# One Mish activation from PSUM in the second mixture, and small VectorE work of the attention on other engines

## The chip, the cores and the metric

The kernel runs on one core of a Trainium2 chip. Its five engines run side by side, each with its own queue that is worked in order: TensorE (PE in the profile; its weight loads are PEld), VectorE (DVE), ScalarE (ACT), GpSimd (POOL) and SyncE (SP), whose queue issues all the transfers here. The metric is device microseconds of one execution; lower is better.

## The reference

Three layers follow each other. B=2, H=8, S=768, D=40, so 1536 tokens of 320 values; the weights come as float64.

```python
for t in range(S):                                   # attention with gates, per batch and head
    m_new = max(f_gate[t] + m, i_gate[t])
    f_stab, i_stab = exp(f_gate[t] + m - m_new), exp(i_gate[t] - m_new)
    C = f_stab * C + i_stab * outer(v[t], k[t])
    n = f_stab * n + i_stab * k[t]
    y[t] = sigmoid(o_gate[t]) * (C @ q[t]) / max(abs(n . q[t]), 1)
x = ((y @ w1) * (y @ w2)) @ w3 @ w_out               # first mixture, 320 -> 1024 -> 320
h = x @ w_in                                         # second mixture, 320 -> 2048 -> 320
out = (h * tanh(softplus(h))) @ w_out2               # h * tanh(softplus(h)) is Mish
```

## The kernel before

**Precision.** Every float32 operand of a large product is split into a high part, rounded to the type that TensorE multiplies at full rate, and a low part, the rest. A product is high x high + high x low + low x high, summed in PSUM. So each activation tile needs a rounding copy and a subtraction.

**Weights.** A weight piece is 128 rows by up to 384 columns of float64 words; there are 80. Each is a chain over four engines (`add_piece`): SP loads the words (`raw`, 4 buffers); `mag` (ACT, an Abs over the high words, L285); `clamp`, `bits1`, `bits2`, `bits` (four DVE passes that put a float32 together, L289, L293, L298, L303); `hi` (ACT rounding copy, L308); `lo` (POOL subtraction, L211, the line of a helper `tt` that issues every two-input operation). The float32 in the middle, `f`, has 5 buffers.

**Attention.** Chunks of 128 steps; a unit `u` is one chunk of all 8 heads of one batch, 12 units. Per unit: `E` (PE exponents) -> `dw` (ACT exp) -> `vw` (POOL) ; `S` (PE scores) -> `wg` (DVE); `I` (PE, what the state gives) -> `Ie` (DVE); `U` (PE) -> `st` (DVE, new state); `Y` (PE) -> `cb`, `r1`, `r2`, `r3` (DVE: sum, magnitude, max with 1, reciprocal) -> `xo` (POOL, three operations) -> `X` (PE transpose) -> `Xe` (ACT), `Xl` (DVE, two operations: low parts). `rb(c)` builds the right-hand factor of the exponents of chunk c on DVE, once per chunk, and `E` waits for it. Products without a use (`keep_warm`, tile `psz`, L369) stand at the start and in the first five units, since TensorE's granted clock falls when it has little to do.

**First mixture.** Tokens stand in 3 blocks of 512. Per block and each of 8 slices of 128 columns: `A` and `B` (8 products of 512 columns each, L747, tiles `psa`, `psb`), `Ae` (ACT copy), `Be` (DVE product of both), `Ph` (ACT), `Pl` (DVE), then `X1` (8 products, L787 to L792, tile `psx`). `W` (L721, tile `psw`) multiplies w3 by w_out beforehand.

**Second mixture.** 48 steps i (3 blocks x 16 slices of 128 columns). `H` (8 products of 512 columns, L747, tile `psh`) -> `He` (copy of PSUM to `h`, the first 18 on ACT, L844, the rest on DVE, L846) -> `Hm` (DVE min with 20, L849) -> `Hx` (ACT Exp, L852) -> `G`, for two steps at a time (ACT Ln of 1 + u for both, L909, then Tanh for both, L911; a load of ScalarE's function table ahead of each pair) -> `gm` (DVE product with `h`), `gh` (DVE rounding copy, L859), `gl` (DVE subtraction) -> `O` (12 products of 320 columns, L874, tile `pso`).

**Order.** `Work` is a list scheduler that runs while the kernel is built: every node has an engine, a due number, a duration that it is thought to last, what it depends on and the buffer places that it takes; on a free engine the node that can start first, and among such the one that is due first, comes next. The due numbers come from `TUNE`. The result is a fixed order in each queue.

Of the kernel before, what the change touches and what calls it, by code (L numbers as in the profile page):

```python
# [10 lines left out]
F32 = mybir.dt.float32  # L11
# [5 lines left out]
# numbers of buffers  # L17
# [8 lines left out]
NUH = 22  # L26
NG_ = 3
GRP = 2
# where the streams of work stand in the order
TUNE = dict(  # L30
    s_pe=0.21, s_act=0.25, s_dve=0, s_pool=0.02, warm=5, ahead=6, w0n=10, he_act=18, a0=132.2, ap=2.52,
    a_ld=-24.1, e_e=289.88, e_s=231.89, e_r=475.63, rb=6, g_ld=-373.09, o_1=-239.57, o_2=520.41, c_ld=-47.15,
    c_wo=548.73, cp_wo=0.032, p0=141.8, pp0=6.543, c_12=-449.5, w0=-140.23, wp=0.004, t_0=-366.73,
    c_w3=-109.65, p1=-597.93, pp1=0.013, p2=-192.0, pp2=621.703, x0=337.71, x_p=-433.57, x1=51.37, x2=-134.49,
    xp=0.002, c_o2=449.63, cp_o2=0.01, c_wi=511.67, c_o3=121.71, m0=987.19, mp0=0.005, mp=1.376, m_o=15.52,
    m_g=228.41, m_t=218.91,
)

# the magnitudes of float32 as the high words of float64, read as float32
# [4 lines left out]
class Work:  # L44
    """Orders the work of the engines: nodes with what they depend on, the places that they take and how long they
    are thought to last; on a free engine the node that is due first comes next."""
# [3 lines left out]
    TABLE = 1.3  # L50
    WINDOW = 3.4133
# [27 lines left out]
    def run(self, t0, fill=None):  # L79
# [15 lines left out]
        def place_of(takes, got):  # L95
            """the place of a list that is free first, or None if none is known to be"""
# [13 lines left out]
        while left:  # L110
# [65 lines left out]
def kernel(  # L176
# [69 lines left out]
    # places of 2 KiB in each partition, the first of them from the start  # L246
# [22 lines left out]
    pieces = []  # L269

    def add_piece(due, lead, width, loads, outs, takes=(), gates=()):
        """outs: functions that give the tiles of the high and the low part, in the places that takes names"""
# [37 lines left out]
        def low():  # L310
# [4 lines left out]
        add_node(("mag", n), "ACT", due - 4, 0.41 * e, mag, [("load", n), ("mag", n - 1)],  # L315
                 [(places("f", NF), [("lo", n)])])
# [8 lines left out]
    def cols_loads(w, ft):  # L325
        """128 columns of a matrix with 384 rows"""
# [28 lines left out]
    # the factors of the exponents, whose rows are high and low parts of 16 rows of gates each  # L355
# [4 lines left out]
    def load_rows(dst, src, u):  # L360
        """the rows of a unit, all heads of one time step side by side"""
# [3 lines left out]
    def keep_warm(n):  # L365
        """products without a use: the tensor engine's clock falls when its array has little to do"""
# [4 lines left out]
    def add_unit(u, due):  # L371
# [10 lines left out]
        def ld_qk():  # L382
            """the columns of a unit, the heads in pairs at partitions 0 and 64"""
# [66 lines left out]
        def state():  # L450
# [43 lines left out]
        def xo():  # L494
# [4 lines left out]
            nc.gpsimd.tensor_copy(out=x[:, DM:3 * T], in_=x[:, R0:DM])  # L499
# [11 lines left out]
        def Xl():  # L511
# [3 lines left out]
            tt(nc.vector, h[64:128, 2, sl], p3[64:128, 2], h[64:128, 2, sl].bitcast(F32), sub)  # L515
# [5 lines left out]
        node("E", "PE", -K["e_e"], 0.87, E, [("lb", int(c > 0)), ("rb", c), ("E", u - 1)],  # L521
             [at("dw"), at("dw"), (places("w", NW), [("Y", u), ("vw", u)])])
        node("dw", "ACT", -K["e_e"] + 1, 0.96, dw, [("E", u)], table=["exp"])
        node("S", "PE", -K["e_s"], 1.75 + wl, S_, [("ld_qk", u), ("E", u), ("Y", u - K["ahead"])], [at("wg"), at("wg")], warm=wl)
        node("wg", "DVE", -3, 1.2, wg, [("S", u), ("dw", u), ("vw", u)])
        if c > 0:
            node("I", "PE", -2, 0.87, inter, [("ld_qk", u), ("st", u - B), ("rb", c)],
                 [(AT, [("Ie", u), ("dx", u)] if more else [("Ie", u)])], warm=0.0)
            node("Ie", "DVE", -1, 0.41, inter_e, [("I", u), ("turn", 1)], [(places("y", 2), [("xo", u)])])
        if more:  # L530
# [4 lines left out]
            node("st", "DVE", -1, 1.0 if c else 0.5, state, [("U", u), ("I", u), ("dx", u)])  # L535
        node("Y", "PE", 0, 1.75 + wl, Y, [("wg", u), ("ld_kv", u)], [at("cb")], warm=wl)
        node("cb", "DVE", 1, 0.41, cb, [("Y", u), ("Ie", u)], [] if c else [(places("y", 2), [("xo", u)])])
        node("r1", "DVE", 1, 0.08, r1, [("cb", u)], [(places("r", 2), [("xo", u)])])
        node("r2", "DVE", 1, 0.08, r2, [("r1", u)])
        node("r3", "DVE", 1, 0.12, r3, [("r2", u)])  # L540
        node("xo", "POOL", 2, 2.0, xo, [("r3", u), ("sgm", kb * B + b)], [(places("x", 2), [("X", u)])])
        node("X", "PE", 3, 0.33, X, [("xo", u)], [at("Xl")], warm=0.0)
        node("Xe", "ACT", 3, 0.37, Xe, [("X", u), ("set", kb)])
        node("Xl", "DVE", 3, 0.54, Xl, [("Xe", u)])
# [23 lines left out]
    def start():  # L568
        G = B * H
        # they stand where the activations come later; the rows of the gates eight times, those of sixteen at 32 n used  # L570
# [37 lines left out]
        def part(c0, c1):  # L608
            """the gates of some chunks: what the exponentials are made of"""
# [22 lines left out]
        def rb(c):  # L632
            e = nc.vector if c < K["rb"] else nc.gpsimd
            sl = slice(c * T, (c + 1) * T)
            tt(e, ex_r[c % 2][64:128], L2[64:128, sl].bitcast(F32).unsqueeze(1).to_broadcast([64, H, T]),
# [45 lines left out]
        for c in range(NCH):  # L681
            add_node(("rb", c), "DVE" if c < K["rb"] else "POOL", K["a0"] + 2 * c * K["ap"] - K["e_r"], 1.13 if c < K["rb"] else 1.86,
# [20 lines left out]
    def add_w3(i, due, due_c):  # L703
# [20 lines left out]
        def Wh():  # L724
            w = w34[r] = w34_tile(r, "w34")
            nc.scalar.copy(w[:, 0:R0], tr[r][:, 0:R0])
            nc.scalar.copy(w[:, 512:512 + R], tr[r][:, R0:DM])

        def Wl():
            w = w34[r]  # L730
            tt(nc.vector, w[:, R0:2 * R0], tr[r][:, 0:R0], w[:, 0:R0].bitcast(F32), sub)
            tt(nc.vector, w[:, 512 + R:640], tr[r][:, R0:DM], w[:, 512:512 + R].bitcast(F32), sub)

        add_node(("W", i), "PE", due, 0.406 * n, W,
                 [("lo", w3_n[i]), ("W", i - 1), *[("lo", wo_n[c0 + c]) for c in range(n)]],
                 [(WB, [("Wl", r)])] if ci == 0 else [])
        if ci == NC3 - 1:
            add_node(("Wh", r), "ACT", due + 1, 0.37, Wh, [("W", i)])
# [279 lines left out]
```

## Time and profile before

| | us |
|---|---|
| median of 3 runs | 475.64 (474.40 to 475.76) |
| span of the profiled execution | 478.8 |
| PE busy / PEld busy | 456.2 / 391.3 |
| DVE busy | 399.6 |
| ACT busy | 295.8 |
| POOL busy | 127.7 |
| mean granted TensorE clock | 0.918 |

The profile holds no separate device time for its execution; its span, from the first instruction to the last, is 3.2 us above the median of the runs. Busy time is the union of an engine's instructions; overlapping matmuls make a busy PE look fuller than it is. The granted clock is given as a share of 2.4 GHz; a stretch at 0.50 ran at 1.2 GHz. Stretches are counted in us from the start of the span.

### The profile page before, as it was taken

How to read it: one execution, taken by the hardware profiler on the slowest of the kernel's cores; microseconds unless marked ns; L12 is line 12 of the kernel's file. 1: busy time of each engine (PE TensorE's matmuls, PEld its weight loads, DVE VectorE, ACT ScalarE, POOL GpSimd, SP SyncE). 2: the span in 40 equal slices, each digit the busy share in tenths (PEclk: the TensorE clock that was granted, in tenths of full speed). 3: DMA queues.
4: the chain of work that ended last, by engine and by line, in shares of the span. 5: the costliest groups of instructions: out<-in, count | busy, mean ns of one | idle time of the engine just before them, and what ended most of it. 6: DMA issues, size and time to landing. Idle time of an engine off the chain costs nothing.

```text
span 478.8 us, 7146 instructions
## 1 busy us (share of the span) xinstructions
PE 456.2 (95%) x2490; PEld 391.3 (82%) x2490; DVE 399.6 (83%) x809; ACT 295.8 (62%) x513; POOL 127.7 (27%) x141
## 2 busy tenths in 40 slices
PE   6999899899899999999999998987999999999997
PEld 4777788788787798988888886776887889999996
DVE  5988996998969668777698886999599988878874
ACT  7453245423226542244355649997799899999990
POOL 3345264452245222232212221226241100000000
PEclk9669655958979999999999999989899999999999
DMA  7915454443412332233323332324120000001001
GB/s 215 288 53 161 149 172 139 124 126 94 126 34 88 120 111 88 89 93 93 98 60 120 100 100 67 100 73 115 50 82 1 27 30 0 1 1 56 0 2 55
DMA packets 31828, 41.93 MB, mean 88 GB/s; under 512 B 2160, under 2 KB 25968, under 8 KB 31792
## 3 DMA queue, kind: packets, MB, share of 16 engines
q1 hardware_dynamic: 31792, 41.48, 28.5%
q8 instruction: 19, 0.31, 0.3%
q14 instruction: 17, 0.14, 0.1%
HBM read 39.50 MB, written 1.97 MB: 87 GB/s over the span
## 4 chain that ended last, share of the span: by engine, by line
PE 63%; DVE 19%; issue 7%; ACT 6%; POOL 2%; DMA 1%; SPq 1%; POOLq 0%; DVEq 0%; ACTq 0%
PE pso L874 12%; PE psh L747 9%; PE psa L747 8%; PE psb L747 7%; PE psw L721 6%; PE psY L471 4%; DVE f L298 3%; PE psS L422 2%; DVE f L289 2%; DVE f L303 2%; PE psz L369 2%; PE psx L788 2%; PE psx L789 2%; PE psx L787 2%; POOL wil L211 2%
## 5 line engine op out<-in xcount | busy, mean ns | idle before, releaser
L747 PE MATMUL psh<-hs,wih 128*128 128x512 f32 x144 | 57.4, 399 | 0.0
L747 PE MATMUL psh<-hs,wil 128*128 128x512 f32 x144 | 49.5, 398 | 3.1 <-POOL wil L211 3.1
L289 DVE TENSOR_SCALAR f<-f 128x384 f32<-128x384 f32 (+2 forms) x80 | 36.8, 463 | 14.0 <-ACT f L285 13.7
L303 DVE SCALAR_TENSOR_TENSOR f<-raw,f 128x384 int32<-128x384 int32 (+2 forms) x80 | 47.0, 592 | 1.0
L285 ACT ACTIVATE f<-raw 128x384 f32<-128x384 f32 (+2 forms) x80 | 41.5, 524 | 10.2 <-DMA raw<-in_w_dram 5.7
L298 DVE SCALAR_TENSOR_TENSOR f<-raw,f 128x384 int32<-128x384 int32 (+2 forms) x80 | 46.7, 589 | 0.9
L874 PE MATMUL pso<-wo,gh 128*128 128x320 f32 x192 | 42.6, 310 | 0.0
L211 POOL TENSOR_TENSOR th<-f,th 128x384 fp32r<-128x384 f32 (+1 forms) x24 | 23.6, 984 | 61.7 <-ACT th L308 51.6
L211 DVE TENSOR_TENSOR u<-u,h 128x512 f32<-128x512 f32 x48 | 35.1, 746 | 4.9 <-ACT u L911 4.9
L747 PE MATMUL psh<-ls,wih 128*128 128x512 f32 x96 | 38.4, 400 | 0.0
L211 DVE TENSOR_TENSOR gl<-u,gh 128x512 fp32r<-128x512 f32 x48 | 32.7, 686 | 4.9 <-PE pso L874 4.2
L747 PEld LDWEIGHTS psh<-hs,wil 128*128 128x128 f32 x144 | 27.7, 193 | 9.5 <-POOL wil L211 3.6
L293 DVE TENSOR_SCALAR f<-f 128x384 int32<-128x384 int32 (+2 forms) x80 | 34.2, 434 | 1.1
L471 PEld LDWEIGHTS psY<-kv,w 128*128 128x128 f32 x192 | 33.6, 256 | 1.5 <-DVE w L211 0.2
L874 PEld LDWEIGHTS pso<-wo,gh 128*128 128x128 f32 x192 | 32.6, 188 | 1.5 <-issue 0.4
L874 PE MATMUL pso<-wo2h,gl 128*128 128x320 f32 x96 | 30.8, 320 | 3.0 <-DVE gl L211 3.0
L747 PE MATMUL psa<-hs,w12h 128*128 128x512 f32 x72 | 30.4, 422 | 3.1 <-DVE hs L211 2.1
L471 PE MATMUL psY<-kv,w 128*128 128x41 f32 x192 | 33.3, 337 | 0.1
L308 ACT CAST th<-f 128x384 fp32r<-128x384 f32 (+1 forms) x24 | 11.5, 480 | 35.3 <-DVE f L303 23.9
L852 ACT ACTIVATE u<-u 128x512 f32<-128x512 f32 x48 | 28.9, 624 | 5.9 <-DVE u L849 5.6
L211 POOL TENSOR_TENSOR wil<-f,wih 128x384 fp32r<-128x384 f32 x16 | 21.5, 1356 | 41.0 <-ACT wih L308 41.0
L747 PEld LDWEIGHTS psh<-hs,wih 128*128 128x128 f32 x144 | 27.8, 193 | 5.0 <-ACT wih L308 0.2
(137 smaller groups left out, 1250.6 us busy)
## 6 DMA issues: line engine op xcount, KB each, us to landing
raw<-in_w_dram SPq DMA_DIRECT2D x32, 384.0 KB
raw<-in_w_out_dram SPq DMA_DIRECT2D x24, 320.0 KB
raw<-in_w_in_dram SPq DMA_DIRECT2D x16, 384.0 KB
kv<-in_kv_dram SPq DMA_DIRECT2D x12, 324.0 KB
qk<-in_qk_dram SPq DMA_DIRECT2D x24, 160.0 KB
raw<-in_w_dram SPq DMA_DIRECT2D x8, 256.0 KB
sg<-in_o_gate_dram SPq DMA_DIRECT2D x12, 160.0 KB
out_dram<-yo SPq DMA_DIRECT2D x12, 160.0 KB
```

The source lines that it names most:

```text
L211: return eng.tensor_tensor(out=o, in0=a, in1=b, op=op)
L285: nc.scalar.activation(out=t["f"].bitcast(F32), in_=t["raw"][:, :, 1].bitcast(F32), func=AF.Abs)
L289: nc.vector.tensor_scalar(out=ff, in0=ff, scalar1=HI_MIN, scalar2=HI_MAX, op0=ALU.max, op1=ALU.min)
L293: nc.vector.tensor_scalar(out=f, in0=f, scalar1=3, scalar2=0x3FFFFFFF, op0=ALU.logical_shift_left, op1=ALU.bitwise_and)
L298: nc.vector.scalar_tensor_tensor(out=f, in0=t["raw"][:, :, 1], scalar=-0x40000000, in1=f, op0=ALU.bitwise_and, op1=ALU.bitwise_or)
L303: nc.vector.scalar_tensor_tensor(out=f, in0=t["raw"][:, :, 0], scalar=29, in1=f, op0=ALU.logical_shift_right, op1=ALU.bitwise_or)
L308: nc.scalar.copy(t["h"], t["f"].bitcast(F32))
L471: nc.tensor.matmul(ps[:, h * VW:(h + 1) * VW], lhsT=t["w"][:, h, :], rhs=t["v"][:, h, :], start=True, stop=True)
L721: nc.tensor.matmul(ps, lhsT=t[a][:, c * 128:(c + 1) * 128], rhs=wo[b], start=(c0 + c + s == 0), stop=(c0 + c == KC - 1 and s == 2))
L747: nc.tensor.matmul(ps, lhsT=a, rhs=b, start=(n == 0), stop=(n == len(seq) - 1))
L852: nc.scalar.activation(out=t["u"], in_=t["u"], func=AF.Exp)
L874: nc.tensor.matmul(ps, lhsT=t[a][:, sl], rhs=wo[b], start=(ft == 0 and n == 0), stop=(ft == KF2 - 1 and n == 2))
```

## The change

Second mixture: `He`, `Hm`, `Hx`, `G`, `gm` and `gh` go. Two ACT activations read the bank of `H` itself: `Mh` writes Mish rounded (`gh`), `Mu` writes it in full (`u`); `gl` subtracts. The bank is free after `Mu`. The pairs of steps go too, and the places of the tiles are laid out anew (8 steps may lie between `Mh` and the end of `O`). `H` waits for the last `B` instead of the last `W`.

Weights: for the 32 pieces of the second mixture (`w_in2`, `w_out2`) `mag` is a DVE bit mask instead of an ACT Abs.

Attention: `r1` is an Abs on ACT; the two half-height products of `st` are one; the second operation of `Xl` goes, and `xo` has a fourth operation on POOL for it; `rb` of chunks 2 to 5 is 8 ACT copies with a scale, one per head, instead of one DVE product.

First mixture: the high part of w3 x w_out is one ACT copy instead of two (the same values, laid out side by side). Order: nearly all due numbers of `TUNE`, some durations of nodes, a factor 1.12 on the durations of DVE nodes, `keep_warm` at the start 10 -> 3 products, in the units 5 -> 6 units, and `S` may now run at most 2 units ahead of `Y`.

```diff
-    s_pe=0.21, s_act=0.25, s_dve=0, s_pool=0.02, warm=5, ahead=6, w0n=10, he_act=18, a0=132.2, ap=2.52,
+    s_pe=0.286, s_act=0.0, s_dve=0.0, s_pool=0.0, warm=6, ahead=2, w0n=3, a0=134.03, ap=1.26,
...
+            if e == "DVE":
+                last *= self.SHARED
...
-            nc.scalar.activation(out=t["f"].bitcast(F32), in_=t["raw"][:, :, 1].bitcast(F32), func=AF.Abs)
+            if abs_act:
+                nc.scalar.activation(out=t["f"].bitcast(F32), in_=t["raw"][:, :, 1].bitcast(F32), func=AF.Abs)
+            else:
+                nc.vector.tensor_single_scalar(out=t["f"], in_=t["raw"][:, :, 1], scalar=0x7FFFFFFF, op=ALU.bitwise_and)
...
-                for rows, e, s_e, _ in halves():
-                    tt(nc.vector, s_e, s_e, t["d"][rows, e::2].unsqueeze(2).to_broadcast([D, HP, VW]), mult)
+                s = st[b].rearrange("a p (e v) -> a (p e) v", e=2)
+                tt(nc.vector, s, s, t["d"].unsqueeze(2).to_broadcast([128, H, VW]), mult)
...
-            nc.vector.scalar_tensor_tensor(out=r, in0=y[:, :, D], scalar=-1.0, in1=y[:, :, D],
-                                           op0=mult, op1=ALU.max)
+            nc.scalar.activation(out=r, in_=y[:, :, D], func=AF.Abs)
...
-            nc.gpsimd.tensor_copy(out=x[:, DM:3 * T], in_=x[:, R0:DM])
+            nc.gpsimd.tensor_copy(out=x[:, DM:3 * T].bitcast(F32R), in_=x[:, R0:DM])
+            tt(nc.gpsimd, x[:, R0:DM], x[:, R0:DM], x[:, DM:3 * T], sub)
...
-            tt(nc.vector, h[64:128, 2, sl], p3[64:128, 2], h[64:128, 2, sl].bitcast(F32), sub)
...
-            e = nc.vector if c < K["rb"] else nc.gpsimd
+            if c >= K["rb"]:
+                for h in range(H):
+                    nc.scalar.activation(out=ex_r[c % 2][64:128, h], in_=L2[64:128, sl].bitcast(F32), func=AF.Copy,
+                                         scale=sel_h[64:128, h:h + 1])
+                return
...
-            nc.scalar.copy(w[:, 0:R0], tr[r][:, 0:R0])
-            nc.scalar.copy(w[:, 512:512 + R], tr[r][:, R0:DM])
+            nc.scalar.copy(w[:, 0:DM], tr[r][:, 0:DM])
...
-        def He():
...
-        def gh():
+        def Mh():
             t["gh"] = z_slot("gh").bitcast(F32R)
-            nc.vector.tensor_copy(out=t["gh"], in_=t["u"])
+            nc.scalar.activation(out=t["gh"], in_=t["ps"], func=AF.Mish)
+
+        def Mu():
+            t["u"] = z_slot("u")
+            nc.scalar.activation(out=t["u"], in_=t["ps"], func=AF.Mish)
...
-        add_node(("H", i), "PE", due, 1.73, Hp, [("lo", wi_n[ft]), ("X1l", kb), ("H", i - 1), ("W", KC * NC3 - 1)],
-                 [(MM, [("He", i)])])
+        add_node(("H", i), "PE", due, 1.82, Hp, [("lo", wi_n[ft]), ("X1l", kb), ("H", i - 1), ("B", NBLK * KF1 - 1)],
+                 [(MM, [("Mu", i)])])
```

## Rows read from the trace of the kernel before

**Rows 1.** Busy time by stage of the span: us of the stretch, then busy us (x instructions) of PE, PEld, DVE, ACT and POOL, the granted clock, the share of the DMA engines and GB/s. The stages are the attention, the first mixture, the second mixture up to where PE runs without gaps, and the rest.

```profile
0.00:139.90 139.90, 130.40 (x827) 107.19 (x827) 121.00 (x262) 57.43 (x110) 57.12 (x77) 0.76 0.48 144
139.90:283.20 143.30, 142.28 (x691) 121.19 (x690) 114.39 (x226) 66.94 (x148) 42.27 (x43) 1.00 0.31 94
283.20:383.50 100.30, 92.09 (x441) 78.06 (x440) 89.34 (x181) 89.46 (x148) 28.28 (x21) 0.95 0.22 68
383.50:475.50 92.00, 91.42 (x537) 84.90 (x536) 74.34 (x142) 82.01 (x108) 0.00 (x0) 1.00 0.03 10
...
sum 478.80, PE 456.20 PEld 391.33 DVE 399.60 ACT 295.85 POOL 127.67; mean PE 91.24 PEld 78.27 DVE 79.92 ACT 59.17 POOL 25.53
```

**Rows 2.** The stretch 283.20 to 383.50 again, of some products alone: first those of L747 (`H`, and one `B`), then those of tile `pso` (`O`), then those of tile `psx` (`X1`). The number behind the first x counts the products.

```profile
283.20:383.50 100.30, 59.66 (x240) 46.29 (x239) 0.95 0.22 68
...
283.20:383.50 100.30, 33.06 (x192) 30.68 (x193) 1.68 (x4) 0.95 0.22 68
...
283.20:383.50 100.30, 2.96 (x9) 1.54 (x8) 1.87 (x3) 1.65 (x3) 0.95 0.22 68
```

**Rows 3.** The chain of work that ended last, in order of time: start us, us, what.

```profile
179.14 18.17 PE psb L747 x80
...
310.87 1.28 ACT L909
312.17 1.15 ACT u L909 x2
313.37 1.25 issue
...
330.17 4.27 POOL wil L211
...
438.24 1.81 PE psh L747 x8
440.05 1.77 PE pso L874 x12
```

**Rows 4.** Who waited for whom in the stretch 283.20 to 383.50: us in total, times, longest us.

```profile
POOL wil L211 <- ACT wih L308: 36.0, 8, 6.8
...
PEld pso L874 <- DVE gl L211: 4.4, 5, 2.1
```

**Rows 5.** The stretch 283.20 to 383.50, of the instructions that write or read tile `u` alone: busy us (x instructions) of DVE and of ACT.

```profile
283.20:383.50 100.30, 45.82 (x78) 38.06 (x65) 0.95 0.22 68
```

**Rows 6.** Groups of DVE instructions in the stretch 283.20 to 383.50: busy us, mean ns of one, idle us ahead of them.

```profile
L211 DVE TENSOR_TENSOR gl<-u,gh 128x512 fp32r<-128x512 f32 x16 | 10.9, 682 | 0.3
L303 DVE SCALAR_TENSOR_TENSOR f<-raw,f 128x384 int32<-128x384 int32 (+1 forms) x21 | 10.9, 526 | 0.1
...
L293 DVE TENSOR_SCALAR f<-f 128x384 int32<-128x384 int32 (+1 forms) x20 | 8.9, 452 | 0.1
...
L846 DVE COPY h<-psh 128x512 f32<-128x512 f32 x10 | 6.8, 682 | 0.3
```

**Rows 7.** Groups of ACT instructions in the same stretch.

```profile
L909 ACT ACT_TABLE_LOAD x10 | 12.8, 1283 | 0.1
L911 ACT ACT_TABLE_LOAD x10 | 12.8, 1283 | 0.2
...
L285 ACT ACTIVATE f<-raw 128x384 f32<-128x384 f32 (+1 forms) x20 | 10.6, 528 | 0.0
...
L844 ACT COPY h<-psh 128x512 f32<-128x512 f32 x18 | 10.0, 578 | 2.3 <-PE psh L747 2.2
```

**Rows 8.** The stretches of the attention behind 20 us in which the clock was granted at 0.50; columns as in rows 1.

```profile
20.00:31.70 11.70, 11.70 (x69) 10.42 (x69) 11.49 (x22) 8.50 (x12) 2.76 (x4) 0.50 0.49 147
...
52.20:82.90 30.70, 30.70 (x158) 26.28 (x159) 26.32 (x61) 12.32 (x22) 13.14 (x17) 0.50 0.50 149
...
96.50:110.20 13.70, 13.70 (x57) 10.93 (x57) 12.48 (x25) 3.27 (x7) 5.69 (x7) 0.50 0.32 95
...
130.70:137.50 6.80, 6.80 (x26) 5.92 (x26) 6.22 (x17) 0.00 (x0) 2.59 (x5) 0.50 0.18 58
```

**Rows 9.** Groups of DVE instructions over the whole span, shapes kept apart (`rb`, the products of `st`, `r1`, `Ie`, the second operation of `Xl`).

```profile
L211 DVE TENSOR_TENSOR ex_r<-gates,sel_h 64x1024 fp32r<-64x1024 f32 x6 | 7.3, 1222 | 1.3 <-PE psI L436 1.2
L211 DVE TENSOR_TENSOR st<-st,d 40x164 f32<-40x164 f32 x16 | 7.0, 439 | 0.3
L485 DVE SCALAR_TENSOR_TENSOR r<-y 128x8 f32<-128x8 f32 x12 | 6.9, 574 | 0.1
...
L211 DVE TENSOR_TENSOR y<-psI,eT 128x328 f32<-128x328 f32 x10 | 5.0, 498 | 0.4 <-ACT d L409 0.2
...
L211 DVE TENSOR_TENSOR hs<-psX,hs 64x128 fp32r<-64x128 f32 x12 | 3.5, 294 | 0.2
```

**Rows 10.** The instructions on tile `r`, of which this is `r1`: duration in ns, least, median and most.

```profile
L485 DVE SCALAR_TENSOR_TENSOR r<-y x12: 167/773/973, 28.0 to 136.2; 128x8 f32<-128x8 f32 x12
```

**Rows 11.** Groups of the whole span, shapes kept apart, for prices of ACT and POOL: a function over 512 columns of SBUF (`Hx`), the copy in `xo`, the exponent of 8 columns, an ACT copy with a scale from a tile.

```profile
L852 ACT ACTIVATE u<-u 128x512 f32<-128x512 f32 x48 | 28.9, 624 | 5.9 <-DVE u L849 5.6
...
L499 POOL COPY x<-x 128x64 f32<-128x64 f32 x12 | 3.6, 302 | 0.8
...
L409 ACT ACTIVATE d<-psI 128x8 f32<-128x8 f32 x8 | 1.4, 178 | 6.2 <-PE psI L436 3.7 <-DVE y L211 2.5
...
L645 ACT ACTIVATE ex_l<-gates,sel_b 64x128 fp32r<-64x128 f32 x2 | 0.7, 395 | 0.0
```

More of the change, by code (lines that the diff above doesn't have):

```diff
@@ L50 @@
     TABLE = 1.3
+    SHARED = 1.12
     WINDOW = 3.4133
@@ L269, with add_piece @@
     pieces = []
-    def add_piece(due, lead, width, loads, outs, takes=(), gates=()):
+    def add_piece(due, lead, width, loads, outs, takes=(), gates=(), abs_act=True):
         n = len(pieces)
@@ L314, in add_piece @@
                  bytes=width * 1024)
-        add_node(("mag", n), "ACT", due - 4, 0.41 * e, mag, [("load", n), ("mag", n - 1)],
-                 [(places("f", NF), [("lo", n)])])
+        add_node(("mag", n), "ACT" if abs_act else "DVE", due - 4, (0.41 if abs_act else 0.35) * e, mag,
+                 [("load", n), ("mag", n - 1)], [(places("f", NF), [("lo", n)])])
         add_node(("clamp", n), "DVE", due - 3, 0.27 * e, clamp, [("mag", n)])
@@ L681, in start @@
         for c in range(NCH):
-            add_node(("rb", c), "DVE" if c < K["rb"] else "POOL", K["a0"] + 2 * c * K["ap"] - K["e_r"], 1.13 if c < K["rb"] else 1.86,
+            add_node(("rb", c), "DVE" if c < K["rb"] else "ACT", K["a0"] + 2 * c * K["ap"] - K["e_r"], 1.13 if c < K["rb"] else 2.2,
                      lambda c=c: rb(c), [("ll", int(c > 0)), ("rb", c - 1)] +
@@ L737, in add_w3 @@
         if ci == NC3 - 1:
-            add_node(("Wh", r), "ACT", due + 1, 0.37, Wh, [("W", i)])
+            add_node(("Wh", r), "ACT", due + 1, 0.4, Wh, [("W", i)])
             add_node(("Wl", r), "DVE", due + 2, 0.47, Wl, [("Wh", r)])
@@ L839, in Hp @@
             mm320(t["ps"], cols(wi_n[ft], "h"), cols(wi_n[ft], "l"), xset["b", kb])
-        def He():
-            t["u"], t["h"] = z_slot("u"), z_slot("h")
-            if i < K["he_act"]:
-                nc.scalar.copy(t["h"], t["ps"])
-            else:
-                nc.vector.tensor_copy(out=t["h"], in_=t["ps"])
-        def Hm():
-            nc.vector.tensor_scalar_min(out=t["u"], in0=t["h"], scalar1=20.0)
-        def Hx():
-            nc.scalar.activation(out=t["u"], in_=t["u"], func=AF.Exp)
-        def gm():
-            tt(nc.vector, t["u"], t["u"], t["h"], mult)
-        def gh():
+        def Mh():
             t["gh"] = z_slot("gh").bitcast(F32R)
-            nc.vector.tensor_copy(out=t["gh"], in_=t["u"])
+            nc.scalar.activation(out=t["gh"], in_=t["ps"], func=AF.Mish)
+        def Mu():
+            t["u"] = z_slot("u")
+            nc.scalar.activation(out=t["u"], in_=t["ps"], func=AF.Mish)
         def gl():
@@ L884, in out_rows @@
             nc.sync.dma_start(out=out[t0:t0 + T, :], in_=y)
[L886 to L898 removed]
+        add_node(("H", i), "PE", due, 1.82, Hp, [("lo", wi_n[ft]), ("X1l", kb), ("H", i - 1), ("B", NBLK * KF1 - 1)],
+                 [(MM, [("Mu", i)])])
+        gp = (GP, [("O", i)])
+        add_node(("Mh", i), "ACT", due + 2, 0.62, Mh, [("H", i)], [gp], table=["mish"])
+        add_node(("Mu", i), "ACT", due + 2, 0.62, Mu, [("Mh", i)], [(UP, [("gl", i)])], table=["mish"])
+        add_node(("gl", i), "DVE", due + 3, 0.69, gl, [("Mu", i), ("gl", i - 1)], [gp])
         end = ft == KF2 - 1
@@ L901, in add_second @@
         if end:
-            takes = [(places("z", 4), [])] * 4
-        add_node(("O", i), "PE", due + K["m_o"], 1.63, O, [("gl", i), ("lo", wo2_n[ft]), ("O", i - 1)], takes)
-        if last:
-            grp = range(g * GRP, i + 1)
-            def G():
-                for n in grp:
-                    nc.scalar.activation(out=mt[n]["u"], in_=mt[n]["u"], func=AF.Ln, bias=1.0)
-                for n in grp:
-                    nc.scalar.activation(out=mt[n]["u"], in_=mt[n]["u"], func=AF.Tanh)
-            add_node(("G", g), "ACT", due + K["m_t"], 1.04 * len(grp), G, [("Hx", n) for n in grp],
-                     table=["ln", "exp"])
+            takes = [(YP, [])] * 4
+        add_node(("O", i), "PE", due + K["m_o"], 1.78, O, [("gl", i), ("lo", wo2_n[ft]), ("O", i - 1)], takes)
     with tc.manual_schedule():
```

69 lines of the change are left out of this document (27 added, 42 removed).

## The prediction

> **What bounds the kernel now.** I read the busy time by stage first. The span has four stages [rows 1]. In the first mixture (139.9 to 283.2) PE is busy for 142.28 of 143.30 us at clock 1.00, and in the last 92.0 us for 91.42: there a product of 512 columns follows the last after 0.227 us (18.17 / 80), 8 of them take 1.81 and the 12 of `O` 1.77 [rows 3]. These two stages are bound by PE, whose useful products the change leaves as they are, so nothing is to be won in them, however much DVE and ACT are relieved. What can move is the second mixture's first 100.3 us, with a clock of 0.95, and the attention's 139.9 us, with 0.76 [rows 1].
>
> In the second mixture's first stretch the reader is to set the work against the time. Its products [rows 2], at the spacing of the steady part, are 240/8 x 1.81 + 192/12 x 1.77 + 8 x 0.227 = 54.3 + 28.3 + 1.8 = 84.4 us. It took 100.3, so 15.9 us are lost. The chain of waits says to whom: it runs through two loads of ScalarE's function table (1.28 and 1.25) and the passes between them, and through the low part of a weight piece (POOL `wil`, 4.27) [rows 3]. POOL waited 36.0 us there for the rounding copy that ACT owes each piece, up to 6.8 at a time [rows 4], and ACT is busy for 89.46 of 100.30 us, DVE for 89.34 [rows 1]. Both engines are full, and the pieces stand in ACT's queue behind the table loads.
>
> In the attention DVE is busy for 121.00 of 139.90 us, but PE is too, 130.40 [rows 1]. Behind 20 us the clock was at 0.50, that is 1.2 GHz, for 11.7 + 30.7 + 13.7 + 6.8 = 62.9 us, and in each of these stretches PE is busy from end to end while DVE has gaps [rows 8]. Two limits thus take turns: PE at half its clock, and DVE.
>
> **The second mixture, part by part.** DVE loses all its work on tile `u` but `gl`, and the copies `h`: 45.82 - 10.9 + 6.8 = 41.7 us in that stretch [rows 5, 6]. It gains the masks. The 32 pieces are not all in it, but 21 pieces were finished there [rows 6]. A mask on every second word is in no row; it lies between `bits1` (452 ns, one input, dense) and `bits` (526, two inputs), below which I see no reason for it to go much. I take 0.45: 21 x 0.45 = 9.5 us, at the upper end 11.0. DVE goes to 89.3 - 41.7 + 9.5 = 57.1 of some 85 us.
>
> ACT loses 38.06 (Exp, Ln, Tanh), 12.8 + 12.8 (tables), 10.0 (`h`) and 10.6 (Abs): 84.3 us [rows 5, 7]. It gains two Mish for each of 29 steps. No row has a Mish. The nearest from below is the copy of the same bank, 578 ns [rows 7]; from above, if it cost as much as the parts that it stands for, the copy and three passes of 624 [rows 11], 2.45 us. I take 0.6, at the lower end, since the 65 instructions of Exp, Ln and Tanh on tile `u` took 38.06 / 65 = 0.59 each [rows 5], whatever the function: 58 x 0.6 = 34.8. ACT goes to 89.5 - 84.3 + 34.8 = 40.0 us. The Trainium skill, "ScalarE: Activation LUTs", section on what happens when an exp activation runs, says that throughput is one element per cycle and lane regardless of function. By it, as an estimate, a Mish costs what the copy costs, and the sum would not change; no run here shows it yet.
>
> A bank is now held for `H`, 1.81, and two Mish, 1.2, and some hops: about 3.4 us. Three banks allow a step every 1.1 us, and PE needs 1.81. That costs nothing at 0.6; it would at the upper price (below).
>
> So neither engine bounds this stretch any more, and PE's 84.4 us does. I don't book all of the 15.9: the pieces still pass DVE, ACT and POOL one after the other, waits such as PEld's for `gl`, 4.4 us [rows 4], shrink but don't vanish, and the new order is unknown to me. I take 13.5 and keep 0 and 15.9 as ends. The rest of the second mixture gives nothing, as PE is full there.
>
> The other edits in the first mixture (one ACT copy less for each of 8 rows of w3 x w_out) lie beside a PE that is busy throughout: nothing, with the 143.30 us of PE as cover.
>
> **The attention, part by part.** DVE loses four `rb`, 4 x 1.222 = 4.9; 16 products of `st` at 439 become 8 of the shape of `Ie`, 498: 7.0 - 4.0 = 3.0; the second operation of `Xl`, 3.5; and `r1`, 12 x 0.574 = 6.9 by its mean [rows 9]. But `r1` takes 167 ns at its least and 773 in the median [rows 10], for 8 columns: most of it is time in which it is held up, and the next DVE instruction may be held up in its place. So `r1` is worth between 2.0 and 6.9, and the sum 13.4 to 18.3; I take 15.
>
> The Trainium skill, "SBUF — State Buffer", section "Who interferes with whom", gives a rule that speaks against the change: DVE and GpSimd share a pair of ports as an exclusive lock, and a DVE operation with two SBUF inputs is blocked for the whole of a GpSimd one. The spread of `r1` agrees with it. By that rule the fourth operation of `xo` takes DVE time back, and with `r1` at its least the sum would be, as an estimate, 13.4 - 12 x 0.302 = 9.8 us; the forecast below would move by some 2 us.
>
> What is added: on ACT 4 x 8 copies with a scale, at most 395 ns each [rows 11], 12.6 us, and 12 small Abs at 178, 2.1 us, beside 57.43 busy of 139.90; on POOL 12 operations of 64 columns at about the copy's 302 ns, 3.6 us, beside 57.12 [rows 1, 11]. Both have room on average. `r2` now waits for ACT, which waits for `cb`: two hops in place of one, and an `rb` block of 8 copies, some 3 us, can stand ahead of it in ACT's queue. Behind `r2` on DVE stands whatever the order puts there, `wg` and `st` among it, for which `Y` and `I` wait. Removed and added `keep_warm` products about cancel (7 fewer at the start, where PE waits for transfers anyway, 4 more in unit 5, up to 2 us).
>
> How much of 15 us reaches the end? Where the clock is at 0.50, PE is the limit and a lighter DVE gives nothing until the clock rises: 62.9 of 139.9 us. In the other 77.0 it counts: 15 x 77.0/139.9 = 8.3, less part of POOL's 3.6; I take 7. Ends: 0, and 18.3 scaled by DVE's share of the stage, 18.3 / (121.0/139.9) = 21.2, when the clock follows.
>
> **Sum.** 13.5 + 7 = 20.5 us. The profiled execution's span of 478.8 goes to 458.3. That span is 3.2 above the median of the runs, 475.6, so the forecast for the median is 455.
>
> **Rivals.** (a) The attention doesn't move, because PE at 0.50 is its limit throughout; for it speak rows 8, where PE has no gap in 62.9 us; against it, DVE's 121.00 of 139.90 [rows 1]. 475.6 - 13.5 = 462.
>
> (b) The attention follows DVE in full, since a lighter DVE leaves PE fewer gaps and the clock stays up: 475.6 - 14.5 - 21 = 440.
>
> (c) Slower, by the clock of the attention alone: the hops through ACT (`r1`, `rb`) open gaps on PE, and of the 77.0 us at or near full clock a part falls to 0.50. Each us of full-clock products that falls costs one more us; from 13.5 on it eats the gain. With 25 us of them: 475.6 - 13.5 + 25 = 487. For it speaks that PE's full-clock stretches are short already; against it, that ACT is busy for 41% of the stage [rows 1].
>
> (d) No change: the second mixture's lost 15.9 us belong to the pieces' chain, which gets a longer DVE part (the masks, 9.5), and the relief elsewhere is cover only: about 475. Speaking for it, the chain through POOL `wil`; against it, that POOL waited for ACT, not ACT for DVE [rows 4]. (A Mish at its upper price would be slower still: two of 2.45 are 4.9 us a step, above PE's 1.81 + 1.77 = 3.58, and 48 steps would take 235 us instead of 172; it decides from 1.79 us a Mish on. I give that 2 in 100, counted with (c).)
>
> **How the numbers follow.** Forecast 0.48 (its own range 448 to 461), (a) 0.22, (b) 0.15, (c) with the dear Mish 0.10, (d) 0.05. The likeliest is 455. The range from 438 to 470 holds the forecast, (a) and most of (b), and leaves out (c), (d) and the far side of (b), together under 2 in 10. A measurement of this kernel tells about 0.3%, 1.4 us, from no change (the runs spread by 1.4). Faster by more: 0.48 + 0.22 + 0.15 and a small part of (d), 0.86; within 0.3%: 0.04; slower: 0.10.
>
> **What would show it.** In the profile after: the second mixture from its first `H` to the steady part shorter by 12 to 16 us, with ACT below 50% busy in it and two Mish of about 0.6 us a step; one table load for them, or very few; POOL's wait for ACT's rounding copies of `wih` far below 36 us. The steady part again 1.81 and 1.77 with PE full. In the attention DVE's busy time lower by 13 to 18 us per same work, and the stage 5 to 10 us shorter, with its half-clock time about as it was. The prediction is wrong if Mish takes over a microsecond, if half-clock time grows beyond 63 us, if gaps turn up on PE in the first mixture, where I booked nothing, or if the new order holds DVE up in front of a wait for ACT.

## The result

The changed kernel has two times. Of 12 executions three took 453 us (452.76, 453.36, 453.52; mean granted clock 0.974) and nine 474 to 476 (clock 0.91 to 0.92); the median of all is 475.46, that of the kernel before 475.69. Ratios here and below go by the executions within 1.5% of a kernel's shortest, and by these three the change makes the kernel faster: ratio 0.953, 95% interval 0.949 to 0.957. But the long times are the kernel's own, nine in twelve, and while they stay unexplained the result is worth little: they eat the whole gain.

The profiled execution is one of the long ones (476.08 us, span 474.3). Its page shows where the clock went: seven of its 40 slices are at five or six tenths of full speed.

```profile
PEclk9659755569959999999999999999999999999999
```

By stage, columns as in [rows 1]; the third and fourth lines together are the second mixture from its first `H` on, split where PE runs without gaps:

```profile
0.00:146.10 146.10, 136.88 (x825) 112.77 (x826) 105.63 (x226) 68.65 (x153) 59.31 (x89) 0.71 0.46 138
146.10:294.90 148.80, 146.96 (x708) 124.21 (x707) 127.10 (x252) 63.91 (x132) 47.49 (x46) 1.00 0.32 98
294.90:340.20 45.30, 43.40 (x229) 38.23 (x228) 41.94 (x82) 24.16 (x45) 16.20 (x12) 1.00 0.31 93
340.20:470.90 130.70, 130.70 (x742) 119.79 (x740) 41.74 (x72) 39.46 (x74) 6.24 (x7) 1.00 0.06 18
...
sum 474.30, PE 457.97 PEld 395.01 DVE 316.97 ACT 196.18 POOL 129.24; mean PE 91.59 PEld 79.00 DVE 63.39 ACT 39.23 POOL 25.85
```

Against [rows 1] the attention is 6.2 us longer although DVE has 15.4 us less to do in it, the first mixture 5.5 longer, and the second mixture, from its first `H` to the end of PE, 176.0 us in place of 192.3. The gain at the end is spent at the beginning.

The profile of the kernel before, from which [rows 1] and [rows 8] are, needs a caution. Of 39 more executions of that kernel with span and clock on record, each took 1.7 to 1.9 us more than its span, and the median span is 474.0 us at a clock of 0.945. A span of 478.8 at 0.918 stands beside the longest of them (478.5, 479.7 and 480.1 us at 0.924, 0.917 and 0.918, which took 480.27, 481.51 and 481.87). So the profiled execution was some 5 us longer than a usual one, and a stage that is shorter than in [rows 1] can owe up to so much to that.

What the short executions look like no profile of this very program shows. Experiment e5 below is the same program with six products more, and it takes the short time always; its stages stand for them:

```profile
0.00:121.90 121.90, 109.92 (x831) 89.91 (x831) 105.99 (x226) 68.82 (x154) 60.44 (x88) 0.92 0.55 165
121.90:271.20 149.30, 147.19 (x708) 124.26 (x707) 127.13 (x253) 63.52 (x131) 47.47 (x47) 1.00 0.31 97
271.20:316.50 45.30, 43.36 (x229) 38.24 (x228) 41.98 (x82) 24.22 (x45) 16.28 (x12) 1.00 0.32 94
316.50:447.20 130.70, 130.70 (x742) 119.79 (x740) 41.75 (x72) 39.49 (x74) 6.23 (x7) 1.00 0.06 18
```

Everything behind the attention is alike to 0.5 us. The two times differ in the attention alone: 146.1 us at a mean clock of 0.71, 121.9 at 0.92, with the same DVE work (105.6 and 106.0).

**Where the clock falls.** PE's instructions around 50 us in the profile after (start us, us, what, and in brackets the wait ahead of it):

```profile
48.47 0.49 PE L509 MATMUL psX<-ident,x 128*128 128x128 f32 x3
50.33 0.51 PE L452 MATMUL psU<-vw,kv 128*40 128x41 f32 x16 [1.37 <-DVE st L212]
50.86 1.12 PE L438 MATMUL psI<-st,qk 128*128 128x82 f32 x8
51.77 0.25 PE L441 MATMUL psI<-ex_r,ones 128*128 128x8 f32 x1
51.95 0.58 PE L427 MATMUL psS<-qk 40*128 40x128 f32 x4
52.47 0.79 PE L374 MATMUL psz<-causal,identr 128*128 128x512 f32 x1
```

`U` of unit 4 waits 1.37 us for `st` of DVE. From 52.2 us on the clock is granted at 0.50 (1.2 GHz); a `psz` product, some 0.5 us before, takes 0.79. It stays there for 51.2 us, in which PE is busy from end to end:

```profile
52.20:103.40 51.20, 51.20 (x262) 42.48 (x261) 31.66 (x74) 22.74 (x54) 19.34 (x27) 0.50 0.39 119
```

The Trainium skill, "TensorE: Matmul & The Clock Gate", section "What's actually happening", says that the throttled state is the default and that activity releases it. This stretch, by the profile busy for 51.20 of 51.20 us and released only at its end, does not bear that out.

**The second mixture.** Groups of ACT, then one of DVE, between 290 and 345 us of the profile after, and two waits of that stretch:

```profile
L850 ACT ACTIVATE gh<-psh 128x512 fp32r<-128x512 f32 x15 | 8.9, 599 | 9.9 <-PE psh L754 6.1 <-PE pso L869 3.8
L854 ACT ACTIVATE u<-psh 128x512 f32<-128x512 f32 x15 | 8.9, 597 | 2.1 <-DVE gl L212 2.0
...
L850 ACT ACT_TABLE_LOAD x1 | 1.3, 1283 | 0.0
```

```profile
L290 DVE TENSOR_SCALAR f<-raw 128x384 int32<-128x384 int32 x10 | 3.5, 351 | 0.0
```

```profile
POOL wil L212 <- ACT wih L313: 27.4, 10, 5.7
POOL wo L212 <- ACT wo L313: 9.6, 4, 3.2
```

A Mish takes 0.60 us, 48 table loads have become one, a mask takes 0.35. ACT is busy for 24.16 of 45.30 us, then for 39.46 of 130.70.

### The profile page after: what moved, and what is told of

It is laid out like the page before. It is cut to its first block, busy times and chain, and to the rows that moved or that the text cites. A ratio compares the mean times of both kernels' runs of the same rounds, so it can differ in the third digit from the quotient of the medians.

```text
span 474.3 us, 6843 instructions
## 1 busy us (share of the span) xinstructions
PE 458.0 (97%) x2498; PEld 395.0 (83%) x2498; DVE 317.0 (67%) x631; ACT 196.2 (41%) x404; POOL 129.2 (27%) x153
## 4 chain that ended last, share of the span: by engine, by line
PE 45%; issue 4%; POOL 2%; DVE 1%; ACT 0%; POOLq 0%; ACTq 0%
PE pso L869 18%; PE psh L754 15%; POOL wil L212 2%; PE psa L754 2%; PE psb L754 2%; PE psx L794 2%; PE psx L796 2%; PE psx L795 2%; PE psw L729 1%; PE psx L798 1%; PE psx L799 1%; DVE pl L212 0%; DVE f L298 0%; DVE f L294 0%; DVE f L308 0%
## 5 line engine op out<-in xcount | busy, mean ns | idle before, releaser
L850 ACT ACTIVATE gh<-psh 128x512 fp32r<-128x512 f32 x48 | 28.6, 599 | 89.0 <-PE psh L754 85.2
L303 DVE SCALAR_TENSOR_TENSOR f<-raw,f 128x384 int32<-128x384 int32 (+2 forms) x80 | 49.8, 623 | 1.6
L308 DVE SCALAR_TENSOR_TENSOR f<-raw,f 128x384 int32<-128x384 int32 (+2 forms) x80 | 47.2, 591 | 1.3
L294 DVE TENSOR_SCALAR f<-f 128x384 f32<-128x384 f32 (+2 forms) x80 | 39.6, 500 | 7.7 <-ACT f L288 7.2
L476 PEld LDWEIGHTS psY<-kv,w 128*128 128x128 f32 x192 | 36.9, 273 | 2.2 <-issue 0.2
L298 DVE TENSOR_SCALAR f<-f 128x384 int32<-128x384 int32 (+2 forms) x80 | 36.7, 461 | 1.3
L476 PE MATMUL psY<-kv,w 128*128 128x41 f32 x192 | 35.5, 350 | 0.0
L729 PE MATMUL psw<-woh,th 128*128 128x320 f32 x128 | 29.2, 312 | 1.8 <-POOL th L212 0.8
L754 PE MATMUL psb<-hs,w12h 128*128 128x512 f32 x72 | 29.2, 405 | 1.4 <-ACT w L409 1.4
L869 PE MATMUL pso<-wo2h,gh 128*128 128x320 f32 x96 | 29.8, 310 | 0.0
L869 PE MATMUL pso<-wo2l,gh 128*128 128x320 f32 x96 | 29.7, 309 | 0.0
```

What stands on the lines that cost most here:

```text
L294: nc.vector.tensor_scalar(out=ff, in0=ff, scalar1=HI_MIN, scalar2=HI_MAX, op0=ALU.max, op1=ALU.min)
L298: nc.vector.tensor_scalar(out=f, in0=f, scalar1=3, scalar2=0x3FFFFFFF, op0=ALU.logical_shift_left, op1=ALU.bitwise_and)
L303: nc.vector.scalar_tensor_tensor(out=f, in0=t["raw"][:, :, 1], scalar=-0x40000000, in1=f, op0=ALU.bitwise_and, op1=ALU.bitwise_or)
L308: nc.vector.scalar_tensor_tensor(out=f, in0=t["raw"][:, :, 0], scalar=29, in1=f, op0=ALU.logical_shift_right, op1=ALU.bitwise_or)
L476: nc.tensor.matmul(ps[:, h * VW:(h + 1) * VW], lhsT=t["w"][:, h, :], rhs=t["v"][:, h, :], start=True, stop=True)
L729: nc.tensor.matmul(ps, lhsT=t[a][:, c * 128:(c + 1) * 128], rhs=wo[b], start=(c0 + c + s == 0), stop=(c0 + c == KC - 1 and s == 2))
```

## The experiments

**The clock, by products all along the attention** (e1 on the kernel after, e2 on the one before). The two places in a unit where a useless product can stand are used in all 12 units, not in six (five) of them:

```diff
-                if p % 2 and warm:
+                if p % 2 and hot:          # hot = u < 12
```

> The changed kernel, the order of its work untouched, with the products without a use in all twelve units of the attention instead of the first six (24 more products of 512 columns, 5 us at 0.227 each). Theory: the attention is held by TensorE's clock, which its profile shows at 0.50 for about 85 of 146 us, and not by VectorE. Then the half-clock time falls below 40 us, the attention to 120 to 130 us, and the kernel comes out at 448 to 458. Rival: VectorE or the hops through ScalarE set the attention's pace, and the clock only fills the gaps they leave. Then the attention keeps its 146 us and the kernel comes out at 474 to 480.

Measured: 478.99 us in the median; five of six executions at 478.8 to 480.1 (clock 0.92), one at 453.62 (0.98). The expectation failed. In the profile the same `U` waits for the same 1.37 us at 50.4 us, the clock falls at 53.0 and stays at 0.50 for 58.0 us, with the added products in it. In five executions of six, products within the units neither prevent the fall nor end it.

> The kernel before, its order untouched, with the same products in all twelve units instead of the first five (28 more, 6 us). If the clock alone holds the attention: 63 us at half clock become less than 30, the attention goes from 140 to 120 to 128 us and the kernel to 456 to 464. If VectorE, 121 of 140 us busy, holds it as I argued for rival (b): no gain, 474 to 482.

Measured: 479.16, ratio 1.002 (0.997 to 1.006). One stretch of the windows, the attention of e2:

```profile
0.00:139.10 139.10, 130.53 (x851) 103.09 (x852) 121.68 (x261) 56.77 (x110) 57.30 (x77) 0.85 0.49 145
```

The mean clock rose from 0.76 [rows 1] to 0.85, and the stage takes 139.1 us in place of 139.9. Why the gain is so small is not shown. DVE, busy for 121.7 us, may be the limit; but the 28 added products take time too (in e6 below, 39 more cost the attention 5.8 us), and they give the program little more clock than it has without them (of e2's twelve executions the mean clock is 0.933 to 0.968, of the kernel before 0.917 to 0.955). That a better clock is worth nothing there does not follow: of the 39 executions of the kernel before, the one at 0.955 took 472.57 us and the one at 0.917 took 481.51.

**Each half of the change alone** (e3: after, with the attention's edits undone; e4: before, with the attention's edits done; each keeps the due numbers of the kernel that it is made from, and its order is planned anew from them).

> The changed kernel with the attention's edits undone (r1, the products of st, the second operation of Xl and rb on VectorE again, three operations in xo); Mish, the masks and the new order numbers stay. My sum: 13.5 us of the gain belong to the second mixture, so 460 to 464, with the second mixture as short as in the changed kernel. If the attention's edits cost time by their hops, less than that: 450 to 458. If VectorE's relief carried the attention: 466 to 476.

Measured: 482.42, ratio 1.013 (1.007 to 1.018). The second mixture is as short as in the kernel after, 173.8 us, but its attention takes 148.8 and its first mixture 152.4:

```profile
0.00:148.80 148.80, 126.52 (x822) 103.04 (x823) 121.28 (x261) 56.80 (x109) 53.01 (x77) 0.76 0.45 135
148.80:301.20 152.40, 149.32 (x709) 126.54 (x708) 128.52 (x258) 65.38 (x133) 48.30 (x47) 0.98 0.32 97
301.20:475.00 173.80, 173.80 (x969) 158.00 (x967) 82.45 (x148) 63.22 (x118) 17.51 (x17) 1.00 0.12 36
```

So the second mixture's gain needs nothing of the attention's edits. The new due numbers with an attention that still has 121 us of DVE work cost 9 us there, the clock falling at 58.5 us for 47.8 us, and 9 more behind it.

> The kernel before with the attention's edits alone (r1 on ScalarE, one product for st, xo with four operations, Xl with one, rb of chunks 2 to 5 on ScalarE), its own order numbers and second mixture. My sum: 7 us less, 466 to 471, VectorE's busy time in the attention 12 to 18 us lower. Rival (a), TensorE's half clock holds the attention: 474 to 477 with VectorE lower all the same. Rival (c), the hops open gaps and the clock falls: over 480.

Measured: 488.35, ratio 1.021 (1.013 to 1.029). The attention ends 6.7 us earlier than in [rows 1], where the sum said 7 (up to 5 of it can be the long execution that [rows 1] shows), the first `H` comes 8 earlier, and the second mixture takes 205 us, not 192. Two of PE's instructions of this stretch, and their waits:

```profile
299.36 0.80 PE L750 MATMUL psh<-hs,wih 128*128 128x512 f32 x1 [5.84 <-ACT h L847]
...
314.63 0.80 PE L750 MATMUL psh<-hs,wih 128*128 128x512 f32 x1 [3.03 <-ACT h L847]
```

`H` waits for `He` in ACT's queue, which still has the table loads in it, and in 290 to 331 us the clock is at 0.71 in the mean (0.50 for 24 us of them). Work that arrives earlier at a stage whose engines are full waits there. Neither half of the change makes the kernel faster alone, in the one order that the due numbers of its kernel give it; other due numbers were not tried.

**The one thin place** (e5: after, with six useless products ahead of `U` of unit 4, where PE waited 1.37 us; everything else in the same order).

```diff
+            if u == 4:
+                keep_warm(6)
             ps = t["U"] = bank("psU")
```

> The changed kernel, order untouched, with six products without a use (1.4 us) ahead of U of unit 4 alone. In its profile TensorE waits 1.37 us at that place for the state and VectorE, right after three transposes and ahead of 16 small products of U, and about a us later its clock falls to 0.50 and stays there for 51.2 us. Theory: what separates the changed kernel's two times, 453 and 475 to 476, is whether the clock falls at this one place. Then most executions come out at 452 to 456 and the profile shows no half-clock stretch between 40 and 100 us. Rival: the clock would fall at the next thin place anyway; then the times stay as they were, most of them 474 to 477, with the fall some us later.

Measured: 454.87, all six executions from 453.28 to 455.75, ratio 0.956 (0.951 to 0.960). The wait is filled:

```profile
47.70 0.49 PE L511 MATMUL psX<-ident,x 128*128 128x128 f32 x3
47.94 1.64 PE L374 MATMUL psz<-causal,identr 128*128 128x512 f32 x6
49.56 0.51 PE L454 MATMUL psU<-vw,kv 128*40 128x41 f32 x16
...
51.61 0.50 PE L374 MATMUL psz<-causal,identr 128*128 128x512 f32 x1
```

and `psz` still takes 0.50 us at 51.61. Six products of 1.64 us together are worth some 21 us, against the 475.96 that the nine long executions of the kernel after have as their median. Whether it is the gap that they close or the work that they add is not told apart here.

**The same with more filling, and edits taken back one by one.** e6 is e1 with three products ahead of `U` in each unit from 3 on; e7 is e3 with the same; e9, e10 and e11 are e6 with attention edits issued on DVE again in the places of the same order (all four; `rb` alone; `r1` alone).

> The changed kernel, order untouched, with products without a use in all twelve units and three more ahead of U from unit 3 on (24 + 21 products, about 10 us at full clock). Theory, the clock must not fall once: every execution between 452 and 458, with the attention between 118 and 126 us. If the extra products lie on the path: 460 to 466. If the clock still falls: 478 and more.

Measured: 457.56, ratio 0.961 (0.956 to 0.966), no execution above 458.7. The attention takes 127.7 us, 5.8 more than in e5: products where none is needed cost their time.

> The changed kernel with the attention's edits undone, and the same products without a use as in the run with all twelve units and U filled. It measures what the attention's edits are worth while the clock is held up. If VectorE bounds the attention then, as rival (b) has it: 10 to 20 us more than that run, 465 to 475, with VectorE 13 to 18 us busier in the attention. If the clock was all: the same time within 3 us.

Measured: 488.69, ratio 1.026 (1.020 to 1.031). The clock fell at 58.4 us, not at `U` but ahead of `E`, which waited for `wg`:

```profile
59.29 0.79 PE L404 MATMUL psE<-causal,identr 128*128 128x512 f32 x1 [3.76 <-DVE w L212]
```

What the attention edits are worth at a good clock it could thus not say; it says that filling one kind of place does not carry over to an order with another.

> The kernel of the run with all twelve units and U filled (457.6 us, clock 0.92 in an attention of 127.7 us), order untouched, but r1, the two products of st, the second operation of Xl and rb of chunks 2 to 5 are issued on VectorE where their nodes stood, and xo has three operations. It prices the attention's edits while the clock is held up. Theory, VectorE is the limit once TensorE's clock is up: VectorE gets 13 to 18 us more, the attention lasts 138 to 146 us and the kernel 468 to 476. Rival, the edits are cover and the order and the clock made the gain: 456 to 461.

Measured: 480.36; executions from 470.62 (clock 0.959) to 488.89 (0.919). In the profile the wait for `st` ahead of `U` of unit 4 is 2.45 us longer than the three products:

```profile
48.32 0.95 PE L374 MATMUL psz<-causal,identr 128*128 128x512 f32 x3
51.71 0.78 PE L455 MATMUL psU<-vw,kv 128*40 128x41 f32 x16 [2.45 <-DVE st L212]
```

and the clock falls at 51.7 for 51.2 us. The best execution is 13 us above e6, at a clock of 0.959 against 0.98, so that 13 is DVE's work and some clock together. Either way DVE's relief also shortens the waits on which the clock hangs. Two of the four edits tried alone, at a clock of 0.98:

> The same kernel with rb of chunks 2 to 5 alone issued on VectorE again (four products at 1.22 us). If VectorE's time passes to the end one for one while the clock is up: 457.6 + 4.9 = 462. If rb is beside the path: 457 to 459. If the clock falls with the first longer wait: over 470.

Measured: 459.78, ratio 0.967 (0.963 to 0.970), 2.2 us above e6, with intervals that just overlap: of the 4.9 us of DVE that `rb` takes, less than half reaches the end, if any.

> The same kernel with r1 alone issued on VectorE again. By its least duration (167 ns) it is worth 2.0 us, by its mean (574 ns) 6.9: 459.6 if the held-up time only moves to the next instruction (the trace after has r2 at 509 ns mean instead of 349), 464.5 if it goes. Rival: the hop to ScalarE and back, 215 ns and two waits a unit, costs as much as r1 did, and the time is 456 to 458.

Measured: 458.66, 1.1 above e6, within the two intervals (0.9643, 0.961 to 0.968). `r1` is worth about a microsecond, if anything, not the 6.9 of its mean durations before. In e11 it does not take 6.9 either; its group in the attention:

```profile
L493 DVE SCALAR_TENSOR_TENSOR r<-y 128x8 f32<-128x8 f32 x12 | 3.2, 275 | 0.2
```

Nor was its held-up time simply handed to `r2`. That instruction, 349 ns in the mean before, is at 509 in the profile after, but at 352 in e6, against which e11 stands (first line after, second e6):

```profile
L493 DVE TENSOR_SCALAR r<-r 128x8 f32<-128x8 f32 x12 | 6.1, 509 | 2.0 <-ACT r L490 2.0
L496 DVE TENSOR_SCALAR r<-r 128x8 f32<-128x8 f32 x12 | 4.2, 352 | 0.4 <-ACT r L493 0.3
```

What holds both up shows in the profile after, where `r2` of one unit starts while an operation of POOL runs and that of the next while POOL is idle:

```profile
53.25 1.00 POOL L212 TENSOR_TENSOR w12l<-f,w12h 128x384 fp32r<-128x384 f32 x1 [1.92 <-ACT w12h L313]
53.29 0.99 DVE L493 TENSOR_SCALAR r<-r 128x8 f32<-128x8 f32 x1
61.21 0.17 DVE L493 TENSOR_SCALAR r<-r 128x8 f32<-128x8 f32 x1
```

The first ends 0.03 us after POOL's operation. So do all 28 of `r1` and `r2` that take over 0.3 us on DVE in the profiles of before, after, e3 and e11. How often it happens depends on what the order puts beside them: `r1` takes 170 ns in the mean in e3.

**The masks** (e8: after, with `mag` on ACT for all pieces again).

```diff
-        ..., abs_act=False)
+        ...)
```

> The changed kernel with the magnitudes of the second mixture's 32 weight pieces by ScalarE's Abs again instead of VectorE's mask; the order is made anew with them. My sum: 32 masks at 0.34 us (measured in the changed kernel) are 11 us of VectorE beside a TensorE that is full, so the second mixture from its first H stays within 2 us of the changed kernel's 176.0. If the masks were needed (Abs in the way of Mish, or a table load for each): 5 us more or table loads in the profile.

Measured: executions of 487.4 to 488.6 (clock 0.91) and one of 468.46 (0.96): 12 and 15 us above the kernel after at either level. ACT's groups from 290 us on, and a wait:

```profile
L288 ACT ACT_TABLE_LOAD x13 | 16.7, 1283 | 0.2
...
L850 ACT ACT_TABLE_LOAD x12 | 15.4, 1283 | 0.2
```

```profile
DVE f L294 <- ACT f L288: 26.2, 14, 3.4
```

Every change between Abs and Mish is a table load of 1.283 us, 27 of them with two at L854, and the second mixture takes 190 us, not 176 (in an order made anew). The Trainium skill, "ScalarE: Activation LUTs", section "Table sets: the hidden batching unit", counts abs among the cheap functions that are in every set; this run shows a load at the changes all the same. Between Exp passes Abs costs none: in the profile after, between 36 and 146 us, 18 Abs of weight pieces stand among 17 Exp of `dw` with two loads in all. The masks are what makes Mish cheap here.

**A better version** (e12: e5, and 11 useless products ahead of `S` of unit 1, where another stretch at 0.50, 10 to 20 us long and 17 in e5, began at 14 to 18 us in all the other profiles).

```diff
+            if u == 1:
+                keep_warm(11)
```

> The changed kernel with six products ahead of U of unit 4 (454.9 us) and eleven more ahead of S of unit 1, where TensorE waits 2.3 us for the first transfers just ahead of a stretch of 17 us at half clock (17.5 to 34.6). If the clock holds through that stretch, its products take about half: 446 to 450. If the clock falls there all the same, or the attention's start waits for transfers and VectorE: 454 to 457.

Measured: **448.51** (445.38 to 449.57, clock 0.98 to 1.00), ratio 0.9425 (0.938 to 0.947), the fastest kernel of this study. Its attention:

```profile
0.00:117.90 117.90, 108.42 (x841) 88.64 (x842) 106.15 (x226) 67.69 (x153) 60.63 (x89) 0.94 0.56 171
```

## Why the prediction was right, and what in it was not

455 us was forecast, and 453 to 455 is what the kernel takes where its clock stays up (452.8 to 453.5 by itself, 454.9 in e5). The direction, the range and the second mixture were right for the reasons given. The attention was not, and that the total agrees so well is in part luck. By the medians (475.69 before, 454.87 in e5) 20.8 us went, where the sum had 20.5: the second mixture gave 2.7 more than was booked, the first mixture took 6.0 that were not booked, and what is left for the attention is some 11 (20.8 + 6.0 - 16.2) in place of 7, an estimate that takes the other two stages as the profiles have them. By the spans of the profiles (478.8 and 450.6), by which the table goes, 28.2 went. Most of the 7.4 between the two lies in the executions that were profiled: that of before was some 5 us longer than a usual one, and that of e5 (453.28) 1.6 shorter than its median. So the 3.2 us that the forecast took off its span were not a fixed distance between span and time, and the 62.9 us of half clock that it held fixed are those of a long execution.

| term | forecast | profile of before against that of e5 | profile of before against that of after, clock fallen |
|---|---|---|---|
| attention | -7 | -18.0 | +6.2 |
| first mixture | 0 | +6.0 | +5.5 |
| second mixture and the last writing | -13.5 | -16.2 | -16.2 |
| sum, by the spans | -20.5 | -28.2 | -4.5 |

**The second mixture** came out as worked: Mish 0.60 us (0.6), one table load (one or few), the steady part again at 1.81 and 1.76 to 1.77, and in the first 86 us ACT busy for 38.6 (40.0 in the sum) and DVE for 64.8 (57.1). One sign did not come: POOL's wait for `wih` is 27.4 us, and the prediction wanted it far below 36. In the first 45.3 us ACT is at 53% and DVE at 93%, yet PE beside them is busy for 43.4. Of the 16.2 us some 1.7 are other work of PE (3.6 us of it lay behind the first `H` before, 1.9 after); like for like it is 14.5. e3 shows the same without the attention's edits. Mis-sized was the mask, 0.35 us against 0.45, which changed nothing. Missed was what the masks are for: the sum had them as a load on DVE with Abs a saving on ACT, and e8 shows that without them the Mish passes would have had 27 table loads among them, some 14 us of the 16.

**The first mixture** was booked at nothing, as PE is full there. PE is full after too, but the stage got longer: PE has 17 products more in it (x708 against x691), 16 of them two groups of `B` that the new order leaves to it from the stages on either side, and 0.8 us more of gaps; its busy time is 4.7 us longer. Of the 5.5 to 6.0 us some 3.6 are thus moved from the stages on either side; the last us or so is not traced. That a full engine can't be shortened held; that its stage can't be lengthened by the order didn't follow.

**The attention** failed at the last step of its sum. The relief of DVE was sized well: 121.00 to 105.63 us, 15.4 against 15. The error was how much of it reaches the end. The prediction held the half-clock time fixed at 63 us and scaled 15 by the rest. The clock is no property of the stage but hangs on single waits in it: behind 20 us, counted as in [rows 8], 80 us at 0.50 in the profile after, 18 in e5. With the clock up the stage shrank, by 18.0 between the profiles and by some 11 by the medians, in either case by more than 7: rival (b)'s direction, if not surely its 21.2. Part of it, 1.8 us, is the group of `B` that moved out. With the clock fallen the stage grew by 6, by rival (c)'s mechanism at another place: one wait of 1.37 us, for `st` on DVE and not for a hop through ACT as (c) had it. Its price, 24 us between the profiles of after and e5, is close to the 25 that (c) reckoned with; from there it gave 475, not 487, since (c) left the attention's own gain out. The prediction had named the growth of half-clock time beyond 63 us as a sign against itself; it came in the profile after, and nine executions of twelve have a mean clock like that profile's.

What DVE's relief and the clock are worth apart from each other is shown only in part. With the clock fallen the relief is worth little: e3, without it, has an attention of 148.8 us at a mean clock of 0.76, the profile after one of 146.1 at 0.71. With the clock up it is worth at most the 13 us of e9's best execution against e6. The clock alone is not priced in the kernel before, since e2's added products cost time too; between the profiles of after and e5, with the same DVE work, it makes the 24 us. Rivals (b) and (c) were put as exclusive; the attention does the one or the other by execution. Why an execution of after falls on one side or the other, with the same order, stays open: no short execution of after or of e1 was profiled.

**`r1`** was bounded by 2.0 and 6.9. e11 gives 1.1, below the lower end and within the noise. The 6.9 was no price of the instruction but of its places in the order before: there it often started beside a running operation of POOL, in the new order seldom (275 ns in the mean, 164 in the median in e11). The Trainium skill, "SBUF — State Buffer", section "Who interferes with whom", has DVE and GpSimd share a pair of ports; the spread of `r1` and `r2` agrees with it, each long one ending with the POOL operation that ran when it started. The 15 us of the sum stood regardless, by the busy time of the whole stage, and that is not the time at the end: `rb` gave some 2.2 of 4.9.

**Two smaller numbers.** Rival (b)'s sum takes 14.5 us for the second mixture where the forecast takes 13.5; with 13.5 it gives 441, not 440. And the 1.4 us that were to tell a change from none came from three runs; 39 later executions of the kernel before lie between 472.57 and 481.87.

**Rivals (a) and (d)** fell: the attention moved both ways, and the second mixture's pieces did not hold it back.

## What to carry to other kernels

A clock level that the profile shows in a stage isn't a constant of that stage: find the wait ahead of each fall, and price a change both ways, with the fall gone and with it longer. Before a profile's rows become the baseline, set its span and clock against the other runs of the same program: this one was of a long execution. Where one program has two times far apart, look for one short wait of TensorE between small products and fill that place; six products at the right one did what some twenty spread over the stage did not. And where an edit looks like a mere exchange of engines (Abs for a mask), ask what it keeps out of the queue of the engine that it leaves.

## What the runs showed of the hardware

- One program, two times: 453 and 475 us. In a long execution the granted clock falls to 0.50 some 2 us after a wait of 1.37 us and stays there for 51.2 us with PE busy throughout; with that wait filled (e5) six executions of six took the short time.
- Mish over 512 columns of PSUM takes 0.60 us, close to the 0.578 of a copy of the same bank [rows 7].
- Abs between Mish passes cost a table load of 1.283 us at each change, 27 in e8; between Exp passes it cost none.
- `r1` and `r2`, 8 columns on DVE, take 0.17 us, or end some 0.03 us after the POOL operation that runs when they start, up to 0.99 us (28 of 28 long ones in four profiles). The mean of `r1` is 574 ns before, 275 in e11 and 170 in e3.
